# Projections as two row halves of TensorE's array, summed by VectorE, in a fused attention and mixture-of-experts kernel

## The chip, the core and the metric

The kernel runs on one NeuronCore of a Trainium2 chip. TensorE (PE in the profile) multiplies and writes sums to PSUM, which has eight banks of 512 fp32 columns; VectorE (DVE) and ScalarE (ACT) read PSUM; GpSimd (POOL) works in SBUF only; DMA queues move data from and to HBM. The metric is the device time of one execution in microseconds.

## What is computed

First an attention over 8 batches, 8 heads, 576 positions and 64 columns a head, with a mask of blocks of 64. Its output, as `x` of 576 x 512 per batch, goes into a mixture of four experts. Each expert is a causal attention of its own with projections of `x`; a gate picks two experts per position.

```python
scores = scale * np.matmul(q, k.transpose(0, 1, 3, 2))       # 64 batch-heads, 576 x 576
mask = block_i >= block_j
attn = softmax(np.where(mask, scores, -1e9))
x = np.matmul(attn, v)                                        # heads side by side: [8, 576, 512]
...
logits = x @ w_gate                                           # best 2 of 4 experts, softmax over the two
for e in range(E):
    q, k, v = x @ wq[e], x @ wk[e], x @ wv[e]                 # 512 -> 64
    a = softmax(np.where(causal, -1e9, scale * (q @ k.T)))
    out += gate_e * (a @ v @ wo[e])                           # 64 -> 512
```

## The kernel before, in words

Heads and experts go in pairs: one of a pair lies on partitions 0 to 63, the other on 64 to 127. There are 48 pair attentions, four per batch of the first attention (kind A) and two per batch of the experts (kind M). The code writes down tasks (`plan.add`), each of a few instructions with an engine or a choice of engines, buffers that it takes (`get`) and frees (`rel`), and the tasks that it follows. `Plan.run` then places them by a model of costs. On PE the order is a table of numbers, `LINE`; on the other engines a table of priorities, `KEYS`, decides among the tasks that are ready, and for a task marked "AD" also whether ACT or DVE does it. What comes out is a fixed program for each engine; on the chip only semaphores hold an instruction back.

PE has four kinds of task, and the names of the tiles tell them apart in a trace:

- **Scores** (mode S; tiles `hl`, `lo`, `raw`, `mops`): the two members of a pair are multiplied at the same time, one on rows 0 to 63 of the array and one on rows 64 to 127, so matmuls stand in twos of shape 64*128, each writing a bank of its own. Fp32 numbers are split into a high and a low part, and three products (low x high, high x high, high x low) are summed in PSUM. Three score tasks make one pair attention, and one of them ends with products of 64 columns.
- **Transposes** (mode T; `id,e`): 64*128 too, two at a time on the two row halves.
- **Attention times values** (mode C; `eTa`, `eTb` with `va`, `vm`, `vz`): all 128 rows, half of the columns, 128*64.
- **Projections** (mode F; `x` with `wh`, `wl`; `y` with `woh`, `wol`): the whole array, 128*128, twelve matmuls of 256 to 320 columns for a piece of q, k or v (`add_qk`, `add_v`), six of 512 columns for a piece of the output (`add_out`). The weights and `x` are split in high and low, with three products for each of the four pieces of 128 rows.

A projection's sum is made in one bank, and one copy on ACT or DVE brings it into SBUF: to `mops` (q and k), `vm` (v and the gate's logits) or `ob` (output). The last 64 positions of a batch (`rows < P` in `add_v`) end with a DVE addition of two halves of one bank, through the tile `vs`.

DVE adds the mask to scores and takes their extremum in one custom instruction, followed by a read of the accumulator into `nm`; ACT then makes the exponentials `e` with `nm` as bias and adds up each row. Both are the way from a score task to its transposes; copies of `eTa` and `eTb` on ACT or DVE lead from those to the products with the values. `MOST` limits how many banks each kind of task may hold (`m`: projections of q, k, v and products with values, `o` and `f`: output, `s` and `a`: scores, `t`: transposes), and `PRICE` is the planner's cost of a change of mode on PE.

Of the kernel before, what the change touches and what calls it, by code (L numbers as in the profile page):

```python
# [12 lines left out]
F32 = mybir.dt.float32  # L13
# [7 lines left out]
P = 128  # L21
# [257 lines left out]

NBANK = 8  # L280

MOST = {"a": 8, "s": 6, "t": 6, "m": 3, "o": 2, "f": 5}
SYNC = mybir.DependencyInfo(mybir.DependencyClass.Sync, mybir.DependencyReason.DATA)
WARM = 5
FEW = 4
# [46 lines left out]
class Plan:  # L332
# [49 lines left out]
    def run(self):  # L382
# [62 lines left out]
        while left:  # L445
            again = True
            while again:
                again = False
                for e in engines:
# [54 lines left out]
                    if e == "P":  # L504
                        if mode != t.mode:
                            c += PRICE[mode + t.mode]
# [855 lines left out]
```

## Time and profile before

| | |
|---|---|
| three timed runs | 579.07, 579.44 (median), 580.24 us |
| span of the profiled execution, first to last instruction | 577.9 us |
| PE busy | 566.2 us, 98% of the span |
| DVE busy | 467.3 us, 81% |
| ACT busy | 432.7 us, 75% |
| POOL busy | 211.0 us, 37% |
| TensorE clock granted | full speed (1.000) |

No separate execution time is listed for the profiled run, so its span stands beside the median: 1.5 us less, which is taken here as what lies around the span. A busy time is the union of an engine's instructions. Matmuls are pipelined, a matmul's own length is longer than its share of the array, and so the pace of a group of matmuls is read from the distance between starts.

### The profile page before, as it was taken

The numbers are of one execution on the slowest core, as the hardware profiler recorded it, in microseconds if no ns is written. First come the engines' busy times: TensorE is split into PE (matmuls) and PEld (weight loads), VectorE is DVE, ScalarE is ACT, GpSimd is POOL, SyncE is SP. The second block draws the span as 40 slices with busy tenths as digits, with TensorE's granted clock in tenths as the row PEclk, the third lists the DMA queues.
The fourth block names the chain that finished last, engine by engine and source line by source line (L and its number), as shares of the span: only waits on it lengthen the run. The fifth ranks groups of instructions, "written<-read, shape, count | busy, mean of one in ns | idle before, by whom it ended". The sixth has DMA issues, their size and how long they took to land.

```text
span 577.9 us, 19767 instructions
## 1 busy us (share of the span) xinstructions
PE 566.2 (98%) x7794; PEld 525.3 (91%) x7794; DVE 467.3 (81%) x1630; ACT 432.7 (75%) x1363; POOL 211.0 (37%) x330
## 2 busy tenths in 40 slices
PE   7899999999999999999999999999999999999996
PEld 5689999999999989999999999999999999999984
DVE  6999789798978789888877878878898889774851
ACT  5888787888767787677877868768778787665743
POOL 2475236434442253322333516164542434120011
PEclk9999999999999999999999999999999999999999
DMA  6555234322543144422173315343253230301042
GB/s 232 170 197 203 94 123 152 105 67 82 166 163 85 64 121 128 140 83 86 62 240 108 105 41 169 98 143 107 65 183 124 85 105 5 118 4 45 2 173 91
DMA packets 29853, 65.51 MB, mean 113 GB/s; under 512 B 9664, under 2 KB 10176, under 8 KB 29760
## 3 DMA queue, kind: packets, MB, share of 16 engines
q1 hardware_dynamic: 24224, 54.51, 29.6%
q10 hardware_dynamic: 5536, 9.73, 4.8%
q8 instruction: 61, 1.00, 0.7%
q14 instruction: 32, 0.26, 0.2%
HBM read 54.01 MB, written 10.22 MB: 111 GB/s over the span
## 4 chain that ended last, share of the span: by engine, by line
PE 95%; DVE 3%; ACT 1%; issue 0%; POOL 0%; ACTq 0%; DVEq 0%; POOLq 0%
PE bank L325 95%; DVE bank L325 1%; DVE eTb L325 1%; ACT e L325 0%; DVE eTa L325 0%; DVE nm L325 0%; DVE x L325 0%; ACT ob L325 0%; DVE r L325 0%; ACTq L325 0%; POOL id masks.py:199 0%; POOL id masks.py:197 0%; DVE rT L325 0%; DVEq L325 0%; POOLq masks.py:199 0%
## 5 line engine op out<-in xcount | busy, mean ns | idle before, releaser
L325 ACT ACTIVATE e<-bank,nm 128x320 f32<-128x320 f32 (+3 forms) x384 | 218.7, 580 | 27.9 <-DVE nm L325 24.2
L325 DVE CUSTOM_DVE_ANT_0 bank<-bank,mask_a 64x64 f32<-64x64 f32 (+4 forms) x320 | 154.6, 505 | 15.3 <-PE bank L325 8.6
L325 PE MATMUL bank<-x,wh 128*128 128x320 f32 (+1 forms) x512 | 105.7, 301 | 0.0
L325 PEld LDWEIGHTS bank<-id,e 64*128 64x128 f32 x2112 | 86.5, 140 | 14.0 <-issue 5.0
L325 PE MATMUL bank<-id,e 64*128 64x64 f32 x2112 | 96.2, 226 | 1.7 <-ACT e L325 1.6
L325 POOL TENSOR_TENSOR lo<-raw,hl 128x320 fp32r<-128x320 f32 x77 | 65.6, 878 | 78.6 <-ACT hl L325 73.1
L325 PEld LDWEIGHTS bank<-x,wh 128*128 128x128 f32 x512 | 82.0, 188 | 4.0 <-issue 2.7
L325 DVE CUSTOM_DVE_ANT_0 bank<-bank,mask_c 64x64 f32<-64x64 f32 (+4 forms) x160 | 77.4, 506 | 7.3 <-PE bank L325 3.7
L325 PE MATMUL bank<-hl,lo 64*128 64x320 f32 (+2 forms) x352 | 79.9, 380 | 0.4 <-DVE eTb L325 0.4
L325 ACT ACTIVATION_READ_ACCUMULATOR e<-bank,nm 128x1 f32 x384 | 78.5, 204 | 0.0
L325 PE MATMUL bank<-x,wl 128*128 128x256 f32 (+1 forms) x256 | 75.7, 296 | 0.0
L325 ACT COPY eTb<-bank 128x512 f32<-128x512 f32 (+1 forms) x111 | 58.9, 557 | 19.4 <-PE bank L325 18.7
L325 PE MATMUL bank<-hl 64*128 64x320 f32 (+2 forms) x352 | 68.0, 313 | 0.0
L325 PE MATMUL bank<-lo,hl 64*128 64x320 f32 (+2 forms) x352 | 67.7, 313 | 0.0
L325 DVE DVE_READ_ACCUMULATOR2_ANT nm<- 128x1 f32 (+1 forms) x480 | 67.0, 139 | 0.0
L325 PEld LDWEIGHTS bank<-eTb,va 128*64 128x64 f32 x1024 | 59.6, 137 | 3.7 <-issue 2.1
L325 PE MATMUL bank<-eTb,va 128*64 128x128 f32 (+2 forms) x1024 | 62.8, 275 | 0.0
L325 DVE TENSOR_TENSOR x<-bank,rs 128x256 f32<-128x256 f32 (+1 forms) x144 | 46.3, 352 | 17.8 <-PE bank L325 15.1
L325 PE MATMUL bank<-wh,x 128*128 128x260 f32 x288 | 59.2, 289 | 0.0
L325 DVE COPY eTb<-bank 128x512 f32<-128x512 f32 (+1 forms) x81 | 51.7, 654 | 9.2 <-PE bank L325 8.3
L325 PEld LDWEIGHTS bank<-wh,x 128*128 128x128 f32 x288 | 46.9, 188 | 2.9 <-issue 1.4
L325 POOL TENSOR_TENSOR x<-x,x 128x256 fp32r<-128x256 f32 (+1 forms) x43 | 34.9, 814 | 36.8 <-ACT x L325 18.6
(116 smaller groups left out, 1170.4 us busy)
## 6 DMA issues: line engine op xcount, KB each, us to landing
va<-in_v_dram SPq DMA_DIRECT2D x32, 576.0 KB
raw<-in_qk_dram SPq DMA_DIRECT2D x31, 576.0 KB
rs<-dr SPq DMA_DIRECT2D x96, 144.0 KB
out_dram<-ob ACTq DMA_DIRECT2D x32, 256.0 KB
raw<-in_w_dram SPq DMA_DIRECT2D x4, 386.0 KB
out_dram<-ob ACTq DMA_DIRECT2D x8, 128.0 KB
dr<-rT SPq DMA_DIRECT2D x48, 16.0 KB
raw<-in_wo_dram SPq DMA_DIRECT2D x1, 512.0 KB
```

The source lines that it names most:

```text
L325: r = f(*args, **kwargs)
```

## The change

Every projection except those of the last batch's output is now issued as matmuls of 64 rows: for each product, one matmul on rows 0 to 63 writes one bank and one on rows 64 to 127 writes another (`halves`). The contraction is thereby cut in two sums. `add_join` brings the first sum to SBUF with the copy that was there before, on ACT or DVE, and then DVE adds the second bank to it in place. A projection holds two banks. These tasks have a mode of their own, X, which the planner counts to the tiling of scores and transposes. `MOST` is 8 for each kind, `PRICE` has other numbers, and `KEYS` and `LINE` are new tables throughout. The last 64 positions of a batch are first joined to 128 rows in `vs`, whose upper part is copied to `vsh`, and the two are added on POOL or DVE; two small tiles of the gate (`cm`, `ce`) now lie in `vs`.

```diff
-MOST = {"a": 8, "s": 6, "t": 6, "m": 3, "o": 2, "f": 5}
+MOST = {"a": 8, "s": 8, "t": 8, "m": 8, "o": 8, "f": 8}
-TILING = {"F": "F", "C": "C", "S": "H", "T": "H"}
+TILING = {"F": "F", "C": "C", "S": "H", "T": "H", "X": "H"}
...
 LINE = [
-    523, 528,
+    521, 527, 526,
 ]
...
+    def halves(mbs, c, n, rows, terms):
+
+        for i, (x_, y_) in enumerate(terms):
+            for g in range(2):
+                gs = slice(64 * g, 64 * g + 64)
+                nc.tensor.matmul(bank(mbs[g])[:rows, c:c + n], lhsT=x_[gs], rhs=y_[gs], start=(i == 0), stop=(i == len(terms) - 1),
+                                 skip_group_check=True)
+
+    def add_join(out_, mbs, n, rows, key, dep, get, rel=(), more=()):
+        a_ = plan.add("AD", cost_ps(n), lambda e: copy_on(e, out_(), bank(mbs[0])[:rows, :n]), key, deps=(dep, *more), get=get, rel=(mbs[0],))
+        return plan.add("D", 70 + 1.04 * n, lambda e: nc.vector.tensor_tensor(out_(), bank(mbs[1])[:rows, :n], out_(), op=OP.add),
+                        key + 0.02, deps=(a_,), rel=(mbs[1], *rel), use=get)
...
-                mb = Buf("bank", 1, "m")
+                mbs = [Buf("bank", 1, "m") for _ in range(2)]
...
-                        nc.tensor.matmul(reg, lhsT=wh[:, c, ws], rhs=xh, start=(c == 0), stop=False)
-                        nc.tensor.matmul(reg, lhsT=wh[:, c, ws], rhs=xl, start=False, stop=False)
-                        nc.tensor.matmul(reg, lhsT=wl[:, c, ws], rhs=xh, start=False, stop=(c == NP - 1))
+                        terms += [(wh[:, c, ws], xh), (wh[:, c, ws], xl), (wl[:, c, ws], xh)]
+                    halves(mbs, 0, n, P, terms)
...
-            done.append(plan.add("AD", cost_ps(260), f1, kc + .1, deps=(t_,), get=(vb,), rel=(mb,)))
+            done.append(add_join(lambda rows=rows, t=t: vm[:rows, t, :], mbs, 260, rows, kc + .1, t_, (vb,)))
...
-                mbs[t], prevs[t] = Buf("bank", 1, "f" if final else "o"), None
+                mbs[t], prevs[t] = [Buf("bank", 1, "f" if final else "o") for _ in range(2 - final)], None
...
-            a = plan.add("AD", cost_ps(DM), f1, kc + .1, deps=(prevs[t],), get=(ob,), rel=(mb,))
+            a = plan.add("AD", cost_ps(DM), f1, kc + .1, deps=(prevs[t],), get=(ob,), rel=(*mb,)) if final else \
+                add_join(lambda rows=rows, ob=ob: ob_[ob.idx][:rows], mb, DM, rows, kc + .1, prevs[t], (ob,))
```

**PE, the first projection of the program.** Before, PE comes to it from transposes (`id` with `e`), and the piece of 256 columns goes to one bank. A row is a matmul's output tile, its operands and its output size.

```order
L325 MATMUL bank_146<-id_65,el_101 128x64
L325 MATMUL bank_145<-id_65,e_95 128x64
L325 MATMUL bank_145<-id_65,e_96 128x64
L325 MATMUL bank_147<-x_115,wh 128x256 x2
L325 MATMUL bank_147<-x_115,wl 128x256
L325 MATMUL bank_147<-x_116,wh 128x256 x2
L325 MATMUL bank_147<-x_116,wl 128x256
```

The same projection in the changed program, where PE comes to it from scores (`hl`, `lo`).

```order
L339 MATMUL bank_145<-hl_77 128x320
L339 MATMUL bank_144<-hl_77 128x320
L339 MATMUL bank_145<-lo_79,hl_77 128x320
L339 MATMUL bank_144<-lo_79,hl_77 128x320
L339 MATMUL bank_144<-x_114,wh 128x256
L339 MATMUL bank_143<-x_114,wh 128x256
L339 MATMUL bank_144<-x_114,wh 128x256
L339 MATMUL bank_143<-x_114,wh 128x256
L339 MATMUL bank_144<-x_114,wl 128x256
L339 MATMUL bank_143<-x_114,wl 128x256
```

Each product is there twice, for two banks, and the task before it is another one.

**DVE, at the first joins.** Before, DVE makes one copy of a projection to `mops` between masks (ISA rows on `bank` with `mask_a`, then the read into `nm`) and other work.

```order
L325 ISA bank_144,nm<-bank_144,mask_a 128x448
L325 ISA nm 128x1
L325 COPY mops_80<-bank_147 128x320
L325 STREAM_TRANSPOSE rT_138<-r_136 128x32
L325 CAST hl_76<-mops_80 128x576
L325 TENSOR_TENSOR wol<-raw_74,woh 128x352
L325 TENSOR_TENSOR lo_78<-mops_80,hl_76 128x288
L325 COPY eTb_107<-bank_146 128x512
```

The changed program at the same place.

```order
L339 COPY mops_80<-bank_144 128x256
L339 ISA bank_143,nm<-bank_143,mask_a 128x448
L339 ISA nm 128x1
L339 TENSOR_TENSOR mops_80<-bank_143,mops_80 128x256
L339 COPY mops_80<-bank_146 128x320
L339 TENSOR_TENSOR mops_80<-bank_145,mops_80 128x320
L339 TENSOR_TENSOR wol<-raw_74,woh 128x336
L339 COPY mops_80<-bank_145 128x320
L339 RECIPROCAL r_135<-r_135 128x10
L339 TENSOR_TENSOR mops_80<-bank_144,mops_80 128x320
```

An addition stands behind each copy, and three joins lie close together.

Over the whole program, the lists of the two orders give these counts. A run is an unbroken series of matmuls of one mode on PE.

| PE, runs and what stands ahead of them | before | after |
|---|---|---|
| projections on the whole array | 51 (32 after scores, 15 after transposes, 4 after values) | 1 |
| projections on row halves | 0 | 83 (45 after scores, 31 after transposes, 7 after values) |
| products with values | 40 | 47 |
| scores | 96 (78 after transposes, 14 after values, 3 after projections) | 113 (41, 15, 56) |
| transposes | 111 (47 after scores, 42 after projections, 22 after values) | 85 (42, 19, 24) |

| DVE instructions | before | after |
|---|---|---|
| additions in joins, 256 / 260 / 320 / 512 columns | 0 | 32 / 40 / 32 / 31 |
| addition `vm<-bank,vs`, 260 columns | 8 | 0 |
| copies of `eTa` and `eTb`, 512 columns | 92 | 70 |
| copies of `mops`, 320 columns | 21 | 13 |
| copies of `ob`, 512 columns | 12 | 16 |

ACT's copies of `eTa` and `eTb` with 512 columns go from 100 to 122, those of `mops` with 320 from 11 to 19.

## Rows read from the trace of the kernel before

**Rows 1.** Page, busy us (share of the span) and instructions of each engine.

```profile
PE 566.2 (98%) x7794; PEld 525.3 (91%) x7794; DVE 467.3 (81%) x1630; ACT 432.7 (75%) x1363; POOL 211.0 (37%) x330
```

**Rows 2.** Windows: busy us of PE, PEld, DVE, ACT, POOL; clock, DMA share, GB/s.

```profile
60.00:540.00 480.00, 479.97 (x6762) 451.44 (x6759) 398.34 (x1388) 367.46 (x1164) 177.60 (x276) 1.00 0.32 103
420.00:435.00 15.00, 15.00 (x198) 13.64 (x194) 14.05 (x49) 12.44 (x46) 5.39 (x9) 1.00 0.53 163
```

**Rows 3.** Waits of PE's weight loads: us in total, times, longest us.

```profile
PEld bank L325 <- ACT e L325: 6.0, 9, 1.7
PEld bank L325 <- ACT eTb L325: 2.1, 4, 0.7
PEld bank L325 <- DVE nm L325: 1.0, 3, 0.4
```

**Rows 4.** Timeline of PE, projection to transposes to scores: start us, us, instruction, count.

```profile
216.30 0.46 PE L325 MATMUL bank<-x,wh 128*128 128x320 f32 x2
216.60 0.31 PE L325 MATMUL bank<-x,wl 128*128 128x320 f32 x1
216.84 0.71 PE L325 MATMUL bank<-id,e 64*128 64x64 f32 x16
217.36 0.40 PE L325 MATMUL bank<-hl,lo 64*128 64x320 f32 x2
217.59 0.31 PE L325 MATMUL bank<-hl 64*128 64x320 f32 x2
217.74 0.31 PE L325 MATMUL bank<-lo,hl 64*128 64x320 f32 x2
217.88 0.28 PE L325 MATMUL bank<-hl,lo 64*128 64x256 f32 x2
...
218.23 0.72 PE L325 MATMUL bank<-raw 64*128 64x64 f32 x8
218.65 0.45 PE L325 MATMUL bank<-hl,lo 64*128 64x320 f32 x2
218.93 0.32 PE L325 MATMUL bank<-hl 64*128 64x320 f32 x2
```

**Rows 5.** Timeline of PE, scores to projection, the first of 32 such places.

```profile
60.99 0.43 PE L325 MATMUL bank<-lo,hl 64*128 64x448 f32 x2
61.36 0.50 PE L325 MATMUL bank<-x,wh 128*128 128x256 f32 x2
61.70 0.28 PE L325 MATMUL bank<-x,wl 128*128 128x256 f32 x1
```

**Rows 6.** Timeline of PE, scores to projection, the last of the 32.

```profile
543.12 0.42 PE L325 MATMUL bank<-lo,hl 64*128 64x448 f32 x2
543.48 0.39 PE L325 MATMUL bank<-wh,x 128*128 128x260 f32 x1
543.70 0.28 PE L325 MATMUL bank<-wl,x 128*128 128x260 f32 x1
```

**Rows 7.** Timeline of PE, projection to transposes, the first of 42 places and the last.

```profile
51.83 0.28 PE L325 MATMUL bank<-x,wl 128*128 128x256 f32 x1
52.03 0.34 PE L325 MATMUL bank<-id,e 64*128 64x64 f32 x4
...
554.95 0.39 PE L325 MATMUL bank<-woh,yl 128*128 128x512 f32 x1
555.26 0.40 PE L325 MATMUL bank<-id,e 64*128 64x64 f32 x6
```

**Rows 8.** Groups of DVE by shape: count, busy us, mean ns, idle before and releaser.

```profile
L325 DVE TENSOR_TENSOR vm<-bank,vs 64x260 f32<-64x260 f32 x8 | 3.4, 420 | 0.5 <-ACT vs L325 0.3
L325 DVE COPY mops<-bank 128x320 f32<-128x320 f32 x21 | 10.3, 490 | 8.0 <-PE bank L325 7.8
L325 DVE COPY ob<-bank 128x512 f32<-128x512 f32 x12 | 8.3, 690 | 2.3 <-PE bank L325 1.9
```

**Rows 9.** Group of ACT by shape, same columns.

```profile
L325 ACT COPY eTb<-bank 128x512 f32<-128x512 f32 x80 | 45.4, 587 | 11.4 <-PE bank L325 10.8
```

More of the change, by code (lines that the diff above doesn't have):

```diff
@@ L285 @@
 FEW = 4
-TILING = {"F": "F", "C": "C", "S": "H", "T": "H"}
-PRICE = {"FC": 100, "FS": 160, "FT": 85, "CF": 155, "CS": 175, "CT": 148, "SF": 155, "SC": 153, "ST": 0,
-         "TF": 135, "TC": 105, "TS": 8}
+TILING = {"F": "F", "C": "C", "S": "H", "T": "H", "X": "H"}
+PRICE = {"FC": 145, "FS": 180, "FT": 115, "FX": 180, "CF": 205, "CS": 200, "CT": 130, "CX": 200, "SF": 195, "SC": 150,
+         "TF": 225, "TC": 173, "TS": 122, "TX": 122, "XC": 150, "XF": 195}
 STAY = 3.99
@@ L505, in run @@
                         if mode != t.mode:
-                            c += PRICE[mode + t.mode]
+                            c += PRICE.get(mode + t.mode, 0)
                         mode = t.mode
@@ L627, in attention_moe @@
     gate = mk("gate", [P, NT, NE])
-    cm = cp.tile([P, NT, NE, NE], F32, name="cm")
-    ce = cp.tile([P, NT, NE, NE], F32, name="ce")
     rk_ = cp.tile([P, NT, NE], F32, name="rk_")
@@ L645, in attention_moe @@
     lg = cp.tile([P, NT, NE], F32, name="lg")
-    vs = cp.tile([64, 260], F32, name="vs")
+    vs = cp.tile([P, 260], F32, name="vs")
+    vsh = cp.tile([64, 260], F32, name="vsh")
+    cm, ce = [vs[:, i_:i_ + NT * NE * NE].rearrange("p (t a c) -> p t a c", t=NT, a=NE) for i_ in (0, NT * NE * NE)]
     x_ = mk("x", [P, 2 * S + 64], F32R)
@@ L873, in add_attention @@
             c_s = sum(4 * WID[t] / 2.4 + 10 if hl is None or t == 0 else 3 * (WID[t] / 2.24 + (8 if last else 4)) for t in ts_)
-            c_s += 174 * last + 25 + (32 if ts_[0] == 0 else 18) + 40 * (hl is None)
+            c_s += 69 * last - 19 + (32 if ts_[0] == 0 else 25) + 40 * (hl is None)
             sdeps = list(odeps if si or ts_[0] > 1 else odeps[:1]) if hl is None else list(hl[1])
@@ L1055, in f_av @@
                     nc.tensor.matmul(dst, lhsT=w_, rhs=src, start=first, stop=last_, skip_group_check=True)
-            prev = plan.add("P", (576, 1024)[ch] * 4 / 2.4 + (42, 42)[ch], f_av, kk,
+            prev = plan.add("P", (576, 1024)[ch] * 4 / 2.4 + (62, 66)[ch], f_av, kk,
                             deps=tuple(evs[ch]) + tuple(vdeps), get=(mb,), mode="C", rel=((ea, eb)[ch], vb))
@@ L1120, in add_qk, with f @@
                 u += 1
-                def f(e, m=m, n=n, c0=c0, mb=mb):
-                    reg = bank(mb)[:, :n]
+                def f(e, m=m, n=n, c0=c0, mbs=mbs):
                     ws = slice(m * P, (m + 1) * P)
+                    terms = []
                     for c in range(NP):
@@ L1127, in f @@
                         xh, xl = xh_[i][:, c0:c0 + n], xl_[i][:, c0:c0 + n]
-                        nc.tensor.matmul(reg, lhsT=wh[:, c, ws], rhs=xh, start=(c == 0), stop=False)
-                        nc.tensor.matmul(reg, lhsT=wh[:, c, ws], rhs=xl, start=False, stop=False)
-                        nc.tensor.matmul(reg, lhsT=wl[:, c, ws], rhs=xh, start=False, stop=(c == NP - 1))
+                        terms += [(wh[:, c, ws], xh), (wh[:, c, ws], xl), (wl[:, c, ws], xh)]
+                    halves(mbs, 0, n, P, terms)
                 t_ = plan.add("P", 12 * (n / 2.24 + 4) + 11, f, key,
                               deps=[d for c in range(NP) for d in wdone[c]] + [d for c in range(NP) for d in X[b, c][1][ch]],
-                              get=(mb, ob), rel=tuple(X[b, c][0] for c in range(NP)))
-                def f1(e, n=n, c0=c0, isq=isq, mb=mb):
-                    copy_on(e, mops[ob.idx][:, S * (not isq) + c0:S * (not isq) + c0 + n], bank(mb)[:, :n])
-                copies.append(plan.add("AD", cost_ps(n), f1, kc, deps=(t_,), get=(ob,), rel=(mb,)))
+                              get=(*mbs, ob), rel=tuple(X[b, c][0] for c in range(NP)), mode="X")
+                copies.append(add_join(lambda n=n, c0=c0, isq=isq: mops[ob.idx][:, S * (not isq) + c0:S * (not isq) + c0 + n], mbs, n, P,
+                                       kc, t_, (ob,)))
             src = slice(Q0, S) if isq else slice(S, 2 * S)
@@ L1155, in add_v @@
             rows, q0 = VROWS[t], P * t
-            mb = Buf("bank", 1, "m")
+            mbs = [Buf("bank", 1, "m") for _ in range(2)]
             kb = k0 + (k1 - k0) * t / NT
@@ L1159, in add_v, with f @@
             chs = [[0], [0], [0, 1], [1], [1, 2]][t]
-            def f(e, rows=rows, q0=q0, mb=mb):
-                reg = bank(mb)[:, :260]
+            def f(e, rows=rows, q0=q0, mbs=mbs):
                 wv = slice(WV0, WN)
+                if rows < P:
+                    for c in range(NP):
+                        i = X[b, c][0].idx
+                        for x__, w__, r_s, st in ((x_[i][:, q0:q0 + P], wh, P, c == 0), (xh_[i][:, q0:q0 + rows], wl, rows, False)):
+                            for g in range(2):
+                                gs = slice(64 * g, 64 * g + 64)
+                                nc.tensor.matmul(bank(mbs[g])[:r_s, 0:260], lhsT=x__[gs], rhs=w__[gs, c, wv], start=st,
+                                                 stop=(c == NP - 1), skip_group_check=True)
+                    return
+                terms = []
@@ L1164, in f @@
                 for c in range(NP):
                     i = X[b, c][0].idx
-                    if rows < P:
-                        nc.tensor.matmul(reg, lhsT=x_[i][:, q0:q0 + P], rhs=wh[:, c, wv],
-                                         start=(c == 0), stop=(c == NP - 1), skip_group_check=True)
-                        nc.tensor.matmul(reg[:rows], lhsT=xh_[i][:, q0:q0 + rows], rhs=wl[:, c, wv],
-                                         start=False, stop=(c == NP - 1), skip_group_check=True)
-                        continue
@@ L1173, in f @@
                     xh, xl = xh_[i][:, q0:q0 + rows], xl_[i][:, q0:q0 + rows]
-                    nc.tensor.matmul(reg, lhsT=xh, rhs=wh[:, c, wv], start=(c == 0), stop=False)
-                    nc.tensor.matmul(reg, lhsT=xh, rhs=wl[:, c, wv], start=False, stop=False)
-                    nc.tensor.matmul(reg, lhsT=xl, rhs=wh[:, c, wv], start=False, stop=(c == NP - 1))
+                    terms += [(xh, wh[:, c, wv]), (xh, wl[:, c, wv]), (xl, wh[:, c, wv])]
+                halves(mbs, 0, 260, P, terms)
@@ L1178, in add_v @@
             t_ = plan.add("P", (12 if rows == P else 8) * (260 / 2.24 + 4) + 9, f, key,
                           deps=[d for c in range(NP) for d in wdone[c]] + [d for c in range(NP) for ch in chs for d in X[b, c][1][ch]],
-                          get=(mb, vb), rel=tuple(X[b, c][0] for c in range(NP)))
-            def f1(e, rows=rows, t=t, mb=mb):
-                copy_on(e, vm[:rows, t, :], bank(mb)[:rows, 0:260])
+                          get=(*mbs, vb), rel=tuple(X[b, c][0] for c in range(NP)), mode="X")
@@ L1185, in add_v @@
             if rows < P:
-                def f0(e, mb=mb):
-                    copy_on(e, vs[0:64, :], bank(mb)[64:128, :260])
-                def f1(e, rows=rows, t=t, mb=mb):
-                    nc.vector.tensor_tensor(vm[:rows, t, :], bank(mb)[:rows, 0:260], vs[0:64], op=OP.add)
-                mb.left = 2
-                sb = Buf("vs", 1)
-                t_ = plan.add("AD", cost_ps(260), f0, kc + .05, deps=(t_,), get=(sb,), rel=(mb,))
-                done.append(plan.add("D", 70 + 1.04 * 260, f1, kc + .1, deps=(t_, *rest), get=(vb,), rel=(mb, sb)))
+                sb = Buf("vs", 4)
@@ L1196, in add_v @@
+                t_ = add_join(lambda: vs, mbs, 260, P, kc + .05, t_, (sb,), (sb,))
+                t_ = plan.add("ADG", cost_sb(260), lambda e: copy_on(e, vsh, vs[64:128]), kc + .07, deps=(t_,), rel=(sb,), port=True)
+                done.append(plan.add("GD", cost_sub(260), lambda e, t=t, rows=rows: (nc.gpsimd if e == "G" else nc.vector).tensor_tensor(
+                    vm[:rows, t, :], vs[0:64], vsh, op=OP.add), kc + .1, deps=(t_, *rest), get=(vb,), rel=(sb,), port=True))
                 continue
-            done.append(plan.add("AD", cost_ps(260), f1, kc + .1, deps=(t_,), get=(vb,), rel=(mb,)))
+            done.append(add_join(lambda rows=rows, t=t: vm[:rows, t, :], mbs, 260, rows, kc + .1, t_, (vb,)))
@@ L1246, in add_v @@
             prev = [plan.add("A" if i in (5, 10) else "D", 205, lambda e, s_=s_: s_(), kb + 0.3, deps=tuple(prev),
-                             get=(gb,) if i == len(steps) - 1 else (), rel=(lgb,) if i == 3 else (), port=True)]
+                             get=(gb,) if i == len(steps) - 1 else (), rel=(lgb,) if i == 3 else (sb,) if i == 7 else (), port=True)]
         gates[b] = (gb, prev[0])
@@ L1263, in add_out @@
             if 0 in pp:
-                mbs[t], prevs[t] = Buf("bank", 1, "f" if final else "o"), None
+                mbs[t], prevs[t] = [Buf("bank", 1, "f" if final else "o") for _ in range(2 - final)], None
             mb = mbs[t]
             def f(e, pp=pp, both=both, rows=rows, q0=q0, mb=mb):
-                reg = bank(mb)[:rows, 0:DM]
+                reg = bank(mb[0])[:rows, 0:DM]
+                terms = []
                 for p in pp:
@@ L1274, in f @@
                         yh, yl = yh_[yb.idx][:, q0:q0 + P], yl_[yb.idx][:, q0:q0 + P]
+                    if not final:
+                        terms += [(yh, woh[:, p, :]), (yh, wol[:, p, :]), (yl, woh[:, p, :])]
+                        continue
                     nc.tensor.matmul(reg, lhsT=yh, rhs=woh[:, p, :], start=(p == 0), stop=False)
@@ L1277, in f @@
                     nc.tensor.matmul(reg, lhsT=yl, rhs=woh[:, p, :], start=False, stop=(p == 1))
+                if terms:
+                    halves(mb, 0, DM, rows, terms)
             chs = ((0,), (0,), (0, 1), (1,), (1,))[t]
@@ L1281, in add_out @@
             prevs[t] = plan.add("P", 3 * 233 * len(pp), f, key, deps=[prevs[t], *wdone["o"]] + need,
-                                get=(mb,) if 0 in pp else (), rel=tuple(Y[b, p][2 if both else 0] for p in pp))
+                                get=(*mb,) if 0 in pp else (), rel=tuple(Y[b, p][2 if both else 0] for p in pp),
+                                mode="F" if final else "X")
             if 1 not in pp:
@@ L1287, in f1 @@
             def f1(e, rows=rows, mb=mb, ob=ob):
-                copy_on(e, ob_[ob.idx][:rows], bank(mb)[:rows, 0:DM])
+                copy_on(e, ob_[ob.idx][:rows], bank(mb[0])[:rows, 0:DM])
             def f2(e, both=both, rows=rows, q0=q0, ob=ob):
```

442 rows, old and new, of tables (KEYS, LINE) are left out of this document.

## The prediction

> **What bounds the kernel now.** I read first the busy times of the page: PE 98% of the span, DVE 81%, ACT 75% [rows 1]. A high share for PE can hide idle array time, so the second view was the table of windows. From 60 to 540 us PE is busy for 479.97 of 480.00 us, while DVE has 398.34 us of work, 83% [rows 2]. The third was the list of waits: PE's weight loads wait 6.0, 2.1 and 1.0 us for the exponentials, the copies of transposes and the masks, 9.1 us in 16 waits [rows 3]. PE is the bound, and DVE and ACT hold it up little. What can shorten the run is array time within PE's busy time, and the fourth view, PE's timeline, shows how much of it goes into changes of shape.
>
> The steady pace comes first. Two whole-array matmuls of 320 columns take 216.30 to 216.60 us, 0.15 us each; two score matmuls on the two row halves together take 217.59 to 217.74 us, again 0.15 us [rows 4]. I use 0.147 us per 320 columns, and other widths in proportion: 0.118 for 256, 0.119 for 260, 0.206 for 448, 0.235 for 512.
>
> **What the change removes.** Entering the whole array from scores, the first place loses 60.99 to 61.36 = 0.37 less 0.206, so 0.16 us, and then 61.36 to 61.70 = 0.34 less 2 x 0.118, so 0.10 us, as the second weights come late: 0.26 us [rows 5]. The last of these 32 places loses 0.36 - 0.206 = 0.15 and 0.22 - 0.119 = 0.10, so 0.25 us [rows 6]. I take 0.26 for these and for the 15 entries from transposes: 47 x 0.26 = 12.2 us. Leaving it for transposes costs 0.20 - 0.118 = 0.08 at the first place and 0.31 - 0.235 = 0.08 at the last [rows 7]; with the 3 exits to scores 45 x 0.08 = 3.6 us. The four entries from values and five exits to them have counterparts after the change and cancel. Removed: 15.8 us.
>
> By contrast scores and transposes, which are both on row halves, follow each other without a gap: sixteen transposes begin at 216.84, in twos, and the scores begin at 217.36, one transposing pace later. Only the second pair of scores is late, 0.23 - 0.147 = 0.083 us [rows 4]. The Trainium skill, "TensorEngine Tiling (Array Packing)", section Key Properties, says that a change of tiling mode drains TensorE and a change of tile within a mode does not. The trace agrees with 0.16 us against none at the boundary itself; by this rule alone projections on halves would have no price of entry, and the time would be that of the cheap end below.
>
> **What it adds on PE.** The number of columns that pass the array stays, since a pair passes at the pace of one whole matmul; the trace has scores of 256, 320 and 448 columns at it, none of 512. An uncertainty of 2 ns on each of some 1,400 pairs is 3 us either way.
>
> - Runs of products with values go from 40 to 47. No view isolates their change of shape; the nearest row is the whole array's 0.26 + 0.08, so 7 x 0.34 = 2.4 us.
> - Entries into projections from transposes, 31 at the 0.083 us of scores: 2.6 us.
> - Entries from scores, 45. Between two score widths there is no loss (217.74 to 217.88 for 320 columns), but after the short 64-column products the next task's second pair is late, 218.65 to 218.93, 0.28 - 0.147 = 0.13 us [rows 4]. One score task in three ends in such products: 15 x 0.13 = 2.0 us.
> - Scores follow transposes 41 times, where it was 78: -37 x 0.083 = -3.1 us. Scores after projections are taken at nothing, like scores after scores.
>
> Sum on PE: -15.8 + 2.4 + 2.6 + 2.0 - 3.1 = -11.9 us. The unknown is the price of entry on halves. If it is nothing everywhere, -15.8 + 2.4 - 3.1 = -16.5. If each of the 76 entries into projections and 56 into scores after them loses the 0.13, it is -16.5 + 9.9 + 7.3 = +0.7. I take the middle one, by the rows nearest to each kind.
>
> **What it adds on DVE and ACT.** There are 135 additions. Prices: 0.420 us for 256 and 260 columns, from the addition at the end of a batch; for 320 and 512 the DVE copies out of PSUM, 0.490 and 0.690 [rows 8]. So 72 x 0.420 + 32 x 0.490 + 31 x 0.690 = 67.3, less the 8 that go, 3.4: 63.9 us. The new tables take 22 copies of 512 columns and 8 of 320 away and add 4 of `ob`: -15.2 - 3.9 + 2.8 = -16.3. DVE gets 47.6 us more at most (its records overlap, so its busy time grows by less), 514.9 us in all, 90% of 569. ACT takes 22 of 0.587 [rows 9], eight narrower ones and loses four, about 13 us: 446 us, 78%. POOL's added copies have 366.9 us of idle time for cover [rows 1].
>
> Can DVE carry that? From 420 to 435 us it is busy 14.05 of 15.00 us, 94%, and PE is busy for all 15.00 [rows 2]. So 90% is no ceiling as such. Without the cover of PE's queue each addition would cost its 0.4 to 0.7 us. But what was one visit becomes two: the join's addition waits for its copy, and behind it on DVE stand masks, for which exponentials and then transposes wait. The second bank is held all that time. How much more PE waits no row shows. The 9.1 us could grow with DVE's ratio of busy to idle time, 467.3 to 110.6 before and 514.9 to 54.1 after, a factor of 2.25: +11.4 us. Or with ACT's, on which 8.1 of the 9.1 end, 432.7 to 145.2 and 446 to 123: a factor of 1.2, +1.8 us. Nothing is added if the new order leaves more distance. I take 3 us, near to ACT's, and keep 0 to 11.4.
>
> The span: 577.9 - 11.9 + 3.0 = 569.0 us; the median of the runs shown lies 1.5 us above the span of the profile, so 570.5 us. Its own range: 577.9 - 16.5 + 1.5 = 562.9 at the low end; 577.9 - 11.9 + 11.4 + 1.5 = 578.9 at the high end.
>
> **The rivals.**
>
> *The joins hold PE up* (slower). Every projection holds two banks, where it held one, until a DVE addition behind a copy has run; scores and transposes then come late for want of a bank or of a mask. For it: DVE at up to 90% and twice the banks. Against it: PE stays busy beside a DVE at 94% [rows 2]. A wait today is 9.1 / 16 = 0.57 us [rows 3]. The gain of 11.9 is gone when 21 of the 135 joins bring one; if one in four does, 34 x 0.57 = 19.4, and the time is 577.9 - 11.9 + 19.4 + 1.5 = 586.9 us. The same page of the Trainium skill, section PSUM Bottleneck, speaks for this rival: tiling makes TensorE faster and not the evacuation of PSUM.
>
> *Entries cost the most they cost anywhere on halves.* Then the sum is +0.7, with 3 for waits 577.9 + 3.7 + 1.5 = 583.1 us. For it: each place where weights change after short matmuls shows it [rows 4]. Against it: wide scores following wide scores show none.
>
> *The cheap end.* No price of entry, no new waits: 562.9 us.
>
> *The halves don't do what they are for.* Should a projection on halves be a change of shape against scores and transposes like the whole array, 76 x 0.26 + 75 x 0.08 = 25.8 us would come on the -16.5: 577.9 + 9.3 + 3 + 1.5 = 591.7 us. Against it: the shape is that of scores, 64*128, and those change to transposes without a gap [rows 4].
>
> **How the numbers follow.** My forecast has a chance of 0.55, the cheap end 0.15, the joins 0.17, the dear entries 0.08, the useless halves 0.05. A measurement tells 0.2% from no change, 1.2 us here, so faster means under 578.3 us. The forecast gives almost all of its 0.55 to that and the cheap end 0.15; the joins' rival has a part with fewer waits that ends even: faster 0.70, same 0.08, slower 0.22. The range runs from just under the cheap end, 561, over the dear entries to 584; what is left out is most of the joins' case and the useless halves, about 0.2.
>
> **What would show it.** Right: in the timeline pairs of `x` with `wh` follow scores without a gap at their first start, and go on at 0.147 us for 320 columns; PE's shares in the windows stay full; DVE's busy time is 490 to 515 us; additions on `mops`, `vm` and `ob` of 0.42 to 0.69 us. Wrong: gaps of 0.16 us ahead of projections, or pairs slower than whole matmuls (then the sum on PE falls); waits of PE for DVE or ACT well above 12 us, or DVE idle while PE waits for a bank (then the joins decide).

## The result and the profile after

The changed kernel takes 570.77 us (median of 4 runs, 570.24 to 573.76) against 579.31 us before: a ratio of 0.9857, with a 95% interval from 0.9833 to 0.9881. Its profiled execution took 571.03 us with a span of 569.2 us, so 1.8 us lie around the span.

The first part of the page of the changed kernel, to be held against [rows 1]:

```profile
PE 556.0 (98%) x9196; PEld 530.1 (93%) x9196; DVE 492.2 (86%) x1705; ACT 441.8 (78%) x1388; POOL 237.5 (42%) x373
```

PE has 10.2 us less busy time, although the page counts 9,196 matmuls and not 7,794. Outside its busy time the span has 569.2 - 556.0 = 13.2 us, where it had 577.9 - 566.2 = 11.7. DVE has 24.9 us more, ACT 9.1. PE's share is 98% as before: the bound has not moved, it has become shorter. The windows say the same for the long middle [rows 2]:

```profile
60.00:540.00 480.00, 479.76 (x8166) 465.47 (x8162) 426.54 (x1478) 382.48 (x1209) 204.65 (x323) 1.00 0.33 104
```

PE is busy for 479.76 of 480.00 us beside a DVE that is at 426.54, 89% of the stretch.

Where PE's time went is to be seen at single places. The timeline of PE in the changed kernel, from scores into a projection (start us, us, instruction, count), which answers to [rows 5, 6]:

```profile
61.15 0.42 PE L339 MATMUL bank<-lo,hl 64*128 64x448 f32 x2
61.35 0.34 PE L339 MATMUL bank<-wh,x 64*128 64x260 f32 x2
61.47 0.34 PE L339 MATMUL bank<-wl,x 64*128 64x260 f32 x2
61.59 0.46 PE L339 MATMUL bank<-wh,x 64*128 64x260 f32 x4
```

The projection begins 0.20 us after the last pair of scores, which at 448 columns is just that pair's pace (0.206), and the next pairs follow at 0.12 us, the pace of 260 columns. The 0.26 us that the first such place cost before are gone here. After short products and after transposes something is left; two more pieces of the same view:

```profile
103.50 0.33 PE L339 MATMUL bank<-mops 64*128 64x64 f32 x4
103.64 0.54 PE L339 MATMUL bank<-x,wh 64*128 64x320 f32 x4
104.02 0.31 PE L339 MATMUL bank<-x,wl 64*128 64x320 f32 x2
...
143.06 0.39 PE L339 MATMUL bank<-x,wh 64*128 64x320 f32 x1
143.09 0.28 PE L339 MATMUL bank<-id,e 64*128 64x64 f32 x2
143.19 0.54 PE L339 MATMUL bank<-x,wh 64*128 64x320 f32 x3
143.44 0.44 PE L339 MATMUL bank<-x,wl 64*128 64x320 f32 x2
```

In both, two pairs of 320 columns take 0.38 us (103.64 to 104.02, 143.06 to 143.44) where the pace makes 0.294: 0.09 us lost. At 143 us the two row halves run apart: one half starts its projection while the other is still transposing. The widest pairs keep the pace too; the output projections in the same view:

```profile
154.10 0.48 PE L339 MATMUL bank<-lo,hl 64*128 64x448 f32 x2
154.30 0.52 PE L339 MATMUL bank<-woh,y 64*128 64x512 f32 x2
154.55 0.50 PE L339 MATMUL bank<-wol,y 64*128 64x512 f32 x2
154.79 0.49 PE L339 MATMUL bank<-woh,yl 64*128 64x512 f32 x2
155.02 0.49 PE L339 MATMUL bank<-woh,y 64*128 64x512 f32 x2
```

A pair takes 0.23 to 0.25 us; 0.235 was the pace reckoned for 512 columns, which no pair of the kernel before had.

The waits of PE's weight loads (us in total, times, longest) in the changed kernel, to be held against [rows 3]:

```profile
PEld bank L339 <- ACT e L339: 6.8, 9, 1.7
PEld bank L339 <- issue: 5.3, 17, 1.3
PEld bank L339 <- ACT eTb L339: 2.0, 6, 0.5
PEld bank L339 <- ACT eTa L339: 1.8, 4, 1.1
...
PEld bank L339 <- DVE yl L339: 1.0, 1, 1.0
PEld bank L339 <- DVE nm L339: 1.0, 3, 0.4
```

The three waits of [rows 3] made 9.1 us and make 9.8. Idle time that nothing but the issue explains, which is taken here to hold a part of the changes of shape, is 5.3 us in 17 places; the same line of the kernel before was:

```profile
PEld bank L325 <- issue: 16.3, 58, 1.3
```

So 11.0 us of idle loading have gone, and 41 of 58 places.

The additions themselves, on DVE (count, busy us, mean ns, then idle time before):

```profile
L339 DVE TENSOR_TENSOR ob<-bank,ob 128x512 f32<-128x512 f32 x31 | 21.3, 688 | 4.3 <-ACT ob L339 3.5
L339 DVE TENSOR_TENSOR mops<-bank,mops 128x320 f32<-128x320 f32 x32 | 15.6, 488 | 7.2 <-ACT mops L339 6.7
```

With those of 256 and 260 columns (0.42 to 0.43 us) they make 67.3 us, just what was reckoned.

### The profile page after: what moved, and what is told of

It is laid out like the page before. It is cut to its first block, busy times and chain, and to the rows that moved or that the text cites. A ratio compares the mean times of both kernels' runs of the same rounds, so it can differ in the third digit from the quotient of the medians.

```text
span 569.2 us, 22766 instructions
## 1 busy us (share of the span) xinstructions
PE 556.0 (98%) x9196; PEld 530.1 (93%) x9196; DVE 492.2 (86%) x1705; ACT 441.8 (78%) x1388; POOL 237.5 (42%) x373
## 4 chain that ended last, share of the span: by engine, by line
PE 88%; DVE 6%; DMA 3%; ACT 2%; issue 1%; SPq 0%; POOL 0%; ACTq 0%; DVEq 0%; POOLq 0%
PE bank L339 88%; DVE bank L339 3%; DMA dr<-rT 1%; DMA rs<-dr 1%; ACT e L339 1%; DVE x L339 0%; DVE nm L339 0%; DVE eTa L339 0%; SPq L339 0%; DVE eTb L339 0%; DVE ob L339 0%; ACT ob L339 0%; DVE vm L339 0%; DVE vs L339 0%; ACT el L339 0%
## 5 line engine op out<-in xcount | busy, mean ns | idle before, releaser
L339 DVE CUSTOM_DVE_ANT_0 bank<-bank,mask_a 128x192 f32<-128x192 f32 (+3 forms) x320 | 154.8, 503 | 13.9 <-PE bank L339 6.7
L339 PE MATMUL bank<-x,wh 64*128 64x256 f32 (+1 forms) x1024 | 107.5, 295 | 0.0
L339 POOL TENSOR_TENSOR lo<-raw,hl 128x320 fp32r<-128x320 f32 x81 | 68.7, 874 | 58.9 <-ACT hl L339 47.6
L339 PE MATMUL bank<-id,e 64*128 64x64 f32 x2112 | 90.0, 224 | 2.0 <-ACT e L339 1.7
L339 PEld LDWEIGHTS bank<-x,wh 64*128 64x128 f32 x1024 | 90.9, 185 | 0.9
L339 PE MATMUL bank<-x,wl 64*128 64x256 f32 (+1 forms) x512 | 85.0, 291 | 0.0
L339 DVE CUSTOM_DVE_ANT_0 bank<-bank,mask_c 128x320 f32<-128x320 f32 (+4 forms) x160 | 77.6, 504 | 7.4 <-PE bank L339 3.4
L339 ACT COPY eTb<-bank 128x512 f32<-128x512 f32 (+1 forms) x120 | 62.5, 564 | 11.9 <-PE bank L339 10.5
L339 PE MATMUL bank<-wh,x 64*128 64x260 f32 x576 | 62.5, 283 | 0.2 <-ACT eTb L339 0.2
L339 PEld LDWEIGHTS bank<-x,wl 64*128 64x128 f32 x512 | 59.6, 185 | 0.0
L339 PEld LDWEIGHTS bank<-wh,x 64*128 64x128 f32 x576 | 56.9, 185 | 0.9 <-ACT eTb L339 0.5
L339 PE MATMUL bank<-wl,x 64*128 64x260 f32 (+1 forms) x320 | 53.2, 279 | 0.0
```

The costliest lines, as they stand in the source:

```text
L339: r = f(*args, **kwargs)
```

## The experiments

All are the changed kernel with one edit, except the two in the old order. Each was timed beside the kernel before on its own chip (579.79 to 580.17 us), and the difference to the changed kernel is taken between the two ratios: (ratio - 0.9857) x 579.3 us. DVE's busy time is that of the page.

| run | time, us | ratio to before, 95% interval | against the changed kernel, us | DVE busy, us |
|---|---|---|---|---|
| changed kernel | 570.77 | 0.9857 (0.9833 to 0.9881) | | 492.2 |
| all projections on the whole array | 596.8 | 1.0288 (1.026 to 1.0315) | +25.0 | 496.9 |
| only the outputs on the whole array | 577.62 | 0.997 (0.9956 to 0.9985) | +6.5 | 493.4 |
| additions of 8 columns | 570.25 | 0.9831 (0.9808 to 0.9854) | -1.5, intervals overlap | 454.1 |
| 128 columns beside the join | 576.1 | 0.9927 (0.99 to 0.9954) | +4.1 | 513.4 |
| 256 or 384 columns beside it | 590.55 | 1.0176 (1.0141 to 1.0211) | +18.5 | 537.2 |
| a quarter more in the join | 588.99 | 1.016 (1.0145 to 1.0175) | +17.6 | 527.3 |
| half more in the join | 599.98 | 1.0351 (1.0328 to 1.0374) | +28.6 | 540.0 |
| doubled in the join | 619.87 | 1.07 (1.066 to 1.074) | +48.8 | 561.8 |
| old order, halves and joins | 614.77 | 1.061 (1.0576 to 1.0643) | +43.6 | 510.8 |
| old order, additions of 8 columns | 611.39 | 1.0547 (1.0526 to 1.0568) | +40.0 | 473.0 |

### Is it the shape? The whole array in the new order

```diff
-        for i, (x_, y_) in enumerate(terms):
-            for g in range(2):
-                gs = slice(64 * g, 64 * g + 64)
-                nc.tensor.matmul(bank(mbs[g])[:rows, c:c + n], lhsT=x_[gs], rhs=y_[gs], start=(i == 0), stop=(i == len(terms) - 1),
-                                 skip_group_check=True)
+        k = len(terms) // 2
+        for i, (x_, y_) in enumerate(terms):
+            nc.tensor.matmul(bank(mbs[i // k])[:rows, c:c + n], lhsT=x_, rhs=y_, start=(i % k == 0), stop=(i % k == k - 1),
+                             skip_group_check=True)
```

The last 64 positions of a batch are split between the banks in a similar way. Banks, joins and every engine's order stay.

> The changed kernel with its order, banks and additions as they are, but each projection's products run on the whole array again: the first half of the products is summed in one bank, the second half in the other. Only the shape of the matmuls differs. If the gain comes from the change of shape that fell away, 76 entries lose about 0.15 us more than now and 75 exits 0.1 to 0.15 us, 18 to 26 us in all: 589 to 597 us. If the gain comes from the new order, and the shape does little, it stays within 2 us of the changed kernel's 570.8.

It came to 596.8 us, 25.0 us above the changed kernel and 2.9% above the kernel before. The shape is worth all of the gain and more: without it the new order, with its two banks and joins, is the worse kernel. Spread over the 151 changes of shape that this order then contains, that is 25.0 / 151 = 0.17 us each, net of what halves lose at the same places. One change in this run's timeline, from a projection of 256 columns to scores:

```profile
73.94 0.28 PE L339 MATMUL bank<-x,wl 128*128 128x256 f32 x1
74.15 0.42 PE L339 MATMUL bank<-hl,lo 64*128 64x320 f32 x2
74.40 0.31 PE L339 MATMUL bank<-hl 64*128 64x320 f32 x2
74.55 0.32 PE L339 MATMUL bank<-lo,hl 64*128 64x320 f32 x2
```

The scores begin 0.21 us after the last projection, 0.09 more than its pace, and the second pair comes 0.25 us after the first, 0.10 more than its pace: 0.19 us for a way out of the whole array. The page and the waits of this run:

```profile
PE 580.2 (97%) x7794; PEld 526.1 (88%) x7794; DVE 496.9 (83%) x1705; ACT 443.1 (74%) x1388; POOL 238.0 (40%) x373
...
PEld bank L339 <- issue: 15.4, 60, 1.4
```

The number of idle places is back at 60, near the 58 of the kernel before. (The microseconds of that line are no measure of the shape alone: the old order on halves, below, has 12.6 us of it, but in 28 places.)

### Does the number of changes set the price? Only the outputs on the whole array

The same edit under `if n == DM`.

> The changed kernel with only the output projections on the whole array, half of the products in each of the two banks. The order has 52 changes between the whole array and row halves in it, where the kernel with all projections on the whole array has 151 for 26 us. If the price of each change is what counts, 52 x 0.172 = 9 us: 578 to 582 us. If the gain hangs on something else of the halves, on the width or on the narrower projections, the outputs alone cost under 4 us or over 15.

577.62 us, 6.5 us above the changed kernel for 52 changes, 0.125 us each. That is 0.4 us below the time expected and 2.5 us short of the expected 9 in the difference of ratios. A third of the changes costs a quarter of the time. The difference is uncertain by about 1.6 us, so that a lower price in the outputs is likely but only just outside the noise, and two runs cannot show a rule.

### Are the additions covered? Additions of 8 columns

```diff
-lambda e: nc.vector.tensor_tensor(out_(), bank(mbs[1])[:rows, :n], out_(), op=OP.add)
+lambda e: nc.vector.tensor_tensor(out_()[:, :8], bank(mbs[1])[:rows, :8], out_()[:, :8], op=OP.add)
```

> The changed kernel with the join's addition cut to 8 columns; what it leaves out is the second half's sum in all other columns. Every wait and every bank stays, 135 additions become about 0.35 us shorter each, some 45 us of VectorE. If VectorE's added work is covered by TensorE, as the forecast has it, at most the 4.5 us of added waits go: 566 to 571 us. If the joins hold TensorE up, 10 us or more go: 561 us or less.

570.25 us. DVE's busy time falls by 38.1 us and the run by no more than the measurement tells: 1.5 us, uncertain by 1.9. In the changed kernel the additions' columns lie beside PE's work, all but 3.4 us of them at most. The page of this run:

```profile
PE 554.9 (98%) x9196; PEld 530.2 (93%) x9196; DVE 454.1 (80%) x1705; ACT 440.5 (78%) x1388; POOL 237.7 (42%) x373
```

PE's busy time is 554.9 against 556.0 us, and the span 567.7 against 569.2.

### How much cover is left? Longer additions

```diff
+        def f_add(e):
+            nc.vector.tensor_tensor(out_(), bank(mbs[1])[:rows, :n], out_(), op=OP.add)
+            nc.vector.tensor_tensor(out_(), out_(), out_(), op=OP.max)
```

> The changed kernel with a second VectorE operation of the same size behind each join's addition (a maximum of the result with itself, which changes nothing), about 45 us more of VectorE, to some 540 us of 570. If VectorE's work is still covered, less than a tenth of it shows: 571 to 575 us. If the cover is nearly used up, more than half of it shows: 593 us or more. In between the slope tells how much of an addition is exposed.

619.87 us, 48.8 us more: the cover is used up. DVE's busy time grew by 69.6 us and not by 45. The 45 is what cutting an addition to 8 columns was expected to save, and it leaves out the part that does not go with the columns: by their rows the additions take 67.3 us, and the second operations 76.9. Two smaller ones, on `out_()[:, :n // 2]` and `[:, :n // 4]`, were to say where the room ends.

> As the doubled addition, but the second operation covers half of the columns: some 40 us more of VectorE where the doubled one added 69.6 us of busy time for 49 us of run time. If VectorE has no room left at all, the same slope of 0.7 holds and the time is about 599 us. If there is room for the first 20 us or so and all beyond shows, it is 575 to 590 us.

> As before with a quarter of the columns, some 25 us more of VectorE. No room left: slope 0.7, about 588 us. Room for it: within 3 us of the changed kernel, 569 to 574 us.

599.98 and 588.99 us: the first of the two expectations in each case, no room, as far as the times go. The busy times read otherwise. From a quarter to a half DVE gains 12.7 us and the run 11.0, from a half to the double 21.8 and 20.2, a slope of 0.87 to 0.93. Drawn back to no loss, the quarter's +35.1 us of DVE meets the changed kernel's time at 35.1 - 17.6 / 0.87 = +15 us. A single slope of 0.7 from zero does not fit; the price of a microsecond rises with the load. Whether it rises at a knee or by degrees no run shows.

These three lengthen DVE's time and the way from a join to its reader together. The next two separate them: nothing waits for the added operation.

```diff
+            k = 2 if n < 320 else 3
+            real.vector.tensor_reduce(junk[:, :k], id32[:, None, :].to_broadcast([P, k, P]), axis=AX.X, op=OP.max)
```

> The changed kernel with a VectorE operation behind each join's addition that nothing waits for and that waits for nothing: a maximum over 256 or 384 columns of a constant in SBUF, into three spare columns. About 50 us of VectorE. The doubled additions lengthened VectorE's time and the way from a join to its reader at once; here only VectorE's time grows. If VectorE's time is what is used up (about 15 us free, then 0.9 us per us), it is about 600 us. If the way from copy over addition to the reader and the held bank is what costs, it is 571 to 580 us.

> The same with 128 columns, about 26 us of VectorE. By VectorE's time alone 580 us, 11 us beyond the 15 free; by the way from join to reader 570 to 573 us.

590.55 us for +45.0 us of DVE, and with `k = 1` 576.1 us for +21.2. Neither expectation holds as it stood. The slope between the two is 14.4 / 23.8 = 0.6, and it too meets the changed kernel's time near +14 us (21.2 - 4.1 / 0.6). So an estimate from straight lines, which no run between 492.2 and 513.4 us of DVE tests, is that about 15 us are free, whichever way they are spent. Beyond, DVE's time costs 0.6 us per us beside the join and 0.9 in it. At nearly the same DVE time, +45.0 beside the join and +47.8 in it, the run differs by 10 us. The longer way from join to reader is the likely reason; the added operations also differ in kind, which was not tested apart. The page of the full one beside the join:

```profile
PE 566.6 (96%) x9196; PEld 530.3 (90%) x9196; DVE 537.2 (91%) x1840; ACT 442.6 (75%) x1388; POOL 237.2 (40%) x373
```

DVE stops at 91% of the span, and PE gives up its 98%. In the doubled join DVE's share is 91% too:

```profile
PE 575.8 (93%) x9196; PEld 531.5 (86%) x9196; DVE 561.8 (91%) x1840; ACT 441.7 (72%) x1388; POOL 239.2 (39%) x373
...
PEld bank L339 <- ACT e L339: 14.3, 28, 1.3
PEld bank L339 <- DVE mops L339: 11.2, 23, 1.2
```

Here PE waits for the joined q and k (`mops`), and longer than before for exponentials; that late masks stand behind those is an inference from the order of the work.

### Is the new order needed? The old tables with halves and joins

`KEYS` and `LINE` of the kernel before; a task that the change adds gets the priority of the task ahead of it plus 0.02.

> Row halves and joins, but with the tables of the kernel before: TensorE's order is the old one, and the added tasks have the priority of the copy ahead of them. If the shape alone brings the gain, 51 runs of projections each lose about 0.3 us less: 565 to 572 us. If the order had to be made for two banks and a join, TensorE waits for them: 575 us or more.

614.77 us, 6.1% above the kernel before and 43.6 us above the changed one. The shape alone does not bring the gain: PE now waits. Its span is 612.8 us and its busy time 568.9, so 43.9 us lie outside it, where the kernel before had 11.7. The same view of waits, and the granted clock of the run's page in 40 slices, in tenths:

```profile
PEld bank L325 <- ACT e L325: 20.6, 28, 2.3
PEld bank L325 <- issue: 12.6, 28, 2.0
PEld bank L325 <- ACT eTb L325: 5.9, 9, 0.8
PEld bank L325 <- ACT eTa L325: 5.6, 10, 1.3
...
PEclk9997999999999999999999999999999999999997
```

Some of the loss is the clock. In the windows from 50 to 55 and 55 to 60 us the granted clock is 0.62 and 0.70, a mix of its levels of 2.4 and 1.2 GHz, and between 46 and 53 us PE had been idle twice, for 2.0 and 3.4 us, waiting for ACT; from 590 to 612 us the clock is 0.82. As an estimate from these windows, at most 10 x 0.34 + 22 x 0.18 = 7.4 of the 43.6 us can be this.

> Row halves in the old order with the join's addition cut to 8 columns; what it leaves out is the second half's sum in all other columns. If the old order loses to VectorE's time, most of the 44 us between 614.8 and 570.8 comes back: under 590 us. If it loses to the chain of copy and addition, to banks that are held and to the order in which they fall, most of it stays: over 600 us.

611.39 us. With DVE's busy time down from 510.8 to 473.0 us only 3.6 of the 43.6 us come back. The columns of the additions are not what the old order loses to. What is left is the sequence in which joins, masks and exponentials fall, by elimination and not by a run of its own. Whether that is banks that are held or the way over two engines stays open: no run changed one without the other. Nor is it PE's order alone, since the priorities of the other engines were the old ones too.

## Why the prediction was right

The forecast was 570.5 us, by a sum of -11.9 us on PE and +3.0 us of new waits.

- **The changes of shape that go, -15.8 us.** The mechanism is shown by the whole-array run: same order, same banks, +25.0 us. The rival of useless halves is the same thing and lay 591.7 - 570.5 = 21.2 us above the forecast, so it was 3.8 us too cheap, uncertain by 2.1; its 25.8 us stood against halves that cost nothing anywhere. The likely reason is in the split of the price. The entries were read at two places and the exits at their first transposes alone. Read at every place in the trace before (the mean of the two row halves where they arrive apart), the 47 entries lose 11.3 us (forecast 12.2) and the 45 exits 6.7 us (forecast 3.6), since behind an exit the second matmuls are late too: by 0.05 us for transposes, which the merged rows of [rows 7] hide, and by 0.10 us for scores. So 18.0 us went and not 15.8.
- **What halves cost in their place.** From wide scores nothing, as forecast, at the place shown. From transposes 0.09 us, forecast 0.083. After products of 64 columns 0.09 us, where the prediction had 0.13: over 15 places 0.6 us too much. These are single places, not a sum.
- **Pairs at the pace of whole matmuls.** Right at the rows shown, 512 columns among them, and in the medians of the two traces: 0.119 us before and 0.118 after for 256 columns, 0.148 and 0.146 for 320, 0.230 and 0.232 for 512. The 3 us of doubt on this term were not needed.
- **More runs of products with values, +2.4 us.** No run isolates it. It stands as an estimate.
- **DVE.** At most 47.6 us more was forecast and a busy time of 490 to 515; it is 492.2, or 24.9 more. The additions and the copies that were counted came out as priced. But DVE's instructions, added up one by one, grew only by 34.3 us, from 568.6 to 602.9: some 13 us of other work left DVE in the new tables, the subtractions that make `lo` (24 to 11 on DVE, 124 to 137 on POOL) and the copies to `vz` (8 to none on DVE, 10 to 22 on POOL) above all, which the prediction did not count. The rest of the difference, 9.4 us, is records that overlap. That the 24.9 us are covered is shown by the thin additions, which took 38.1 us away and gained nothing that can be told.
- **New waits, +3.0 us.** The three waits that the prediction scaled grew by 0.7 us only. The other added waits are small ones for `eTa`, `yl`, `ob` and `x`; the named waits of the weight loads sum to some 4.5 us more than before. Loads run beside matmuls, and outside PE's busy time the span grew by 1.5 us only. The place was not the one scaled, and the size was half of it.
- **The rival that the joins hold PE up** did not happen at this load but is close. The prediction argued from 15 us at 94% that DVE's 90% was no ceiling. Over the whole run the limit lies lower: with 513.4 us of DVE, 89% of its span, the run with 128 columns beside the join already lost 4.1 us. With its own upper price of 514.9 us the kernel would have stood there, and the rival would have had its share. So the argument from the one dense window was too weak for what it carried. That DVE ended at 492.2 is owed in good part to work that moved to POOL, and this was not foreseen.

By the spans the sum closes: 577.9 to 569.2 us is -8.7 us, the forecast -8.9. That is closer than its terms. PE's busy time fell by 10.2 us where the sum had 11.9, and the rest of the span grew by 1.5 us where it had 3.0; by difference, 18.0 us went and 7.8 came back on PE, where 15.8 and 3.9 had been put. The mechanism is right; that the time came out within 0.3 us is partly luck.

## What to carry to other kernels

Where matmuls of different shapes alternate on TensorE, count the changes of shape in its order and price one from the starts around it, the second matmul behind the change included: here 0.14 to 0.25 us each, in and out, which PE's busy share of 98% hid. Running the odd task in its neighbours' shape paid here even though it needs a second bank and an addition, because the engine that adds had room; and that room is to be measured by adding work to it, since taking work away shows nothing while another engine is the bound. Such a change can want its order made anew: with the old one the same edit lost 6%.

## What the runs showed that was not expected

The limit shows on one side only. DVE at 454 or 492 us gives the same run time, at 513 the run has lost 4.1 us, and from 527 to 562 nearly each further microsecond in the join's way is paid (0.87 to 0.93). In a program whose engines each have a fixed order, an engine at 89% of the span can have nothing left. And a dependent operation of 64 to 128 columns behind an addition takes 0.28 to 0.35 us on DVE, as its rows in the run with a quarter more show:

```profile
L339 DVE TENSOR_TENSOR mops<-mops 128x64 f32<-128x64 f32 x32 | 10.3, 322 | 1.1
L339 DVE TENSOR_TENSOR ob<-ob 128x128 f32<-128x128 f32 x31 | 10.4, 336 | 1.1
```

In the run with half more the same two have twice the columns and take 385 and 482 ns: about 1 ns a column, so some 0.2 us and more of each are the same whatever the width. How much of this is the wait for the result just written is not shown. The independent maximum over 128 columns, which is another operation, takes 276 ns.
